# Attention-and-expert kernel: kv products moved into the group of narrow products, spare weight loads put between wide ones

## The chip, the cores and the metric

The kernel runs on one core of one Trainium2 chip. A core has TensorE (PE; its weight loads are shown apart as PEld), VectorE (DVE), ScalarE (ACT), GpSimd (POOL) and SyncE (SP, which mostly issues DMAs). The metric is device time in microseconds of one execution.

## The reference

x has 2048 rows of 640 columns. Two blocks are added to x: linear attention on the normalized rows, and eight rows ("gated rows") that pass through a small gated MLP.

```python
phi = lambda t: jnp.where(t > 0, t + 1, jnp.exp(t)) + 1e-6
pq, pk = phi(q), phi(k)                                  # 32 heads of 20
kv = jnp.einsum("bhsd,bhse->bhde", pk, v)
z = jnp.einsum("bhsd->bhd", pk)
num = jnp.einsum("bhqd,bhde->bhqe", pq, kv)
den = jnp.einsum("bhqd,bhd->bhq", pq, z)[..., None] + 1e-6
attention = (num / den) @ wo

r = x @ w_r                                              # scores of the rows
idx = jnp.argsort(-r, axis=-1)[:, :8]
y = (silu(x[idx] @ w_gate) * (x[idx] @ w_up)) @ w_down * sigmoid(r[idx])
out = x + attention(layernorm(x)) + (x + scatter of y into rows idx)
```

## The kernel before

The 2048 rows are 16 tiles of 128; D = 640 is five chunks of 128. The program is written by hand as one list of calls; each call issues its instructions to its engines in that order, and each engine works its own list in order. Nothing reorders the calls. The stages, by TensorE:

- **Tiles, about 7 to 52 us.** For each tile t: `K(t)` (line 204) makes keys from the transposed normalized rows `xnT` in two halves of 320 columns, five products each. ACT takes exp and relu of a half, DVE joins them into `pk`. `G(t)` (line 245) then multiplies the tile's rows with `pk` and adds up over all tiles in PSUM: for each of five chunks a product of 512 columns, and for four of them one of 128 columns with the same weights. So kv need not have v: kv is worked out later from G and the v part of the weights. From tile 4 on the order is K(t), then G(t-1).
- **q, about 50 to 78 us.** `q_pe(tb, m, bank)` (line 472) makes queries for 512 rows and one fifth m of the columns: five products of 512 columns, weights from `wq` with a column step of five (`by5`), then exp and relu on ACT. There are 4 x 5 groups. `q_fin` joins exp and relu into `pqT` on DVE. Three PSUM banks go round.
- **Between the q groups** stand narrow products, whose weights have 32 columns and which run four side by side in the array (shape 128*32 in the profile): `kv_pe` (line 613) makes kv from G and `wv`; `den` the denominators; `gu_pe` gate and up of the gated rows; `m_tiled` and `m_edge` the products M of kv and wo, left half of the columns first ("left M", h = 0). A head has 20 columns, so heads straddle the 32-row blocks: `kv_ev` (line 629) masks kv on DVE into `kv1` (the main part) and `kv2` (the edge part), and POOL makes copies of kv2 turned by 32, 64 and 96 rows, which `m_edge` reads. `m_ev0` copies left M from PSUM to `Mb`.
- **Gated rows.** `route2` finds the eight rows and lets POOL gather them into `xsT`; `gu_pe`, `gu_act`, `gu_ev` make `hh`; `ht_pe` (line 708) transposes hh and copies it to `hT`; `y_pe` multiplies with w_down.
- **Output, about 78 to 103 us.** `norm` divides pqT by the denominators, `out_mm` multiplies it with `Mb` (lines 735 to 741), `out_ev` adds x and sends the rows out.

A product is two instructions on TensorE, a load of the weights (LDWEIGHTS, shown in PEld) and the product itself (MATMUL).

The calls around kv in the list of before are

```python
    q_pe(0, 3, 1)
    q_fin(0, 2)
    kv_pe(3)
    kv_ev(3)
    q_pe(0, 4, 0)
```

and those of left M, further down, are `m_tiled(0)`, `q_fin(2, 2)`, `den(0, 3, 0)`, `gu_pe(6)`, `m_edge(0)`.

Of the kernel before, what the change touches and what calls it, by code (L numbers as in the profile page):

```python
# [7 lines left out]
P = 128  # L8
# [7 lines left out]
NG = 4  # L16
# [13 lines left out]
BF16 = mybir.dt.bfloat16  # L30
# [4 lines left out]
ALU = mybir.AluOpType  # L35
# [3 lines left out]
def kernel(  # L39
# [13 lines left out]
    pe, dve, act, pool, sp = nc.tensor, nc.vector, nc.scalar, nc.gpsimd, nc.sync  # L53
# [11 lines left out]
    PS = psp.tile([P, 8, 512], F32, name="PS")  # L65
# [16 lines left out]
    zero = st([P, 512], BF16, "zero")  # L82
# [3 lines left out]
    bm2 = st([P, GC], BF16, "bm2")  # L86
# [33 lines left out]
    def warm4(w):  # L120
# [6 lines left out]
        out=ident[:], in_=ident[:], compare_op=ALU.not_equal, fill=1.0,  # L127
# [9 lines left out]
    kv2 = st([P, NG, GC], BF16, "kv2")  # L137
# [65 lines left out]

    def K(t, hs=(0, 1), b=6, ks=range(KC)):
        for h in hs:
            w = HW + h
            for kc in ks:
                pe.matmul(  # L208
                    PS[:, b + h, off(t, h) : off(t, h) + w],
                    lhsT=xnT[:, kc, t * P : (t + 1) * P],  # L210
                    rhs=wkh[h][:, kc, 0:w],
                    start=(kc == 0),
                    stop=(kc == KC - 1),
                )
# [26 lines left out]
    def PHb(t):  # L241
        ek, rk = phis[t]
        dve.scalar_tensor_tensor(out=pk[:, t, :], in0=ek[:], scalar=1.0, in1=rk[:], op0=ALU.min, op1=ALU.add)  # L243

    def G(t, ks=range(KC)):
        for a in ks:
            lhsT = XX[:, t, 0, a * P : (a + 1) * P]
            pe.matmul(  # L248
                PS[:, a, :], lhsT=lhsT, rhs=pk[:, t, 0:512],
                start=(t == 0), stop=(t == T - 1),  # L250
            )
            if a < 4:
                pe.matmul(  # L253
                    PS[:, 5, a * P : (a + 1) * P], lhsT=lhsT, rhs=pk[:, t, 512:D],
                    start=(t == 0 and a == 0), stop=(t == T - 1), skip_group_check=True,
                )
# [215 lines left out]
    def q_pe(tb, m, bank):  # L472
        for kc in range(KC):
            pe.matmul(  # L474
                PS[:, bank, :], lhsT=by5(wq[:, kc, :])[:, m, :], rhs=xnT[:, kc, tb * TBLK : (tb + 1) * TBLK],
                start=(kc == 0), stop=(kc == KC - 1),
            )
        e = tmp.tile([P, D], BF16, tag="ek", name="qe", bufs=3)[:, 0:TBLK]
        r = tmp.tile([P, D], BF16, tag="rk", name="qr", bufs=3)[:, 0:TBLK]
        act.activation(e, PS[:, bank, :], AF.Exp)  # L480
        act.activation(r, PS[:, bank, :], AF.Relu)  # L481
        qst[(tb, m)] = (e, r)
# [41 lines left out]
    Mb = st([P, KC, WS], BF16, "Mb", "wkM")  # L524
    rd_d = drp.tile([2, H, 8 * P], BF16, name="rd_d")

    def q_fin(tb, m):
        e, r = qst[(tb, m)]
        dve.scalar_tensor_tensor(  # L529
            out=pqT[:, m, tb * TBLK : (tb + 1) * TBLK], in0=e, scalar=1.0, in1=r,  # L530
            op0=ALU.min, op1=ALU.add,
        )

    def den(u, bank, o0):
        for m in range(KC):
            for j in range(4):
                o = (4 * u + j) * 2 * P
                pe.matmul(  # L538
                    PS[32 * j : 32 * j + 32, bank, o0 : o0 + 2 * P], lhsT=zm[:, m, :], rhs=pqT[:, m, o : o + 2 * P],
                    start=(m == 0 and o0 == 0), stop=(m == KC - 1), skip_group_check=True,  # L540
                )
# [69 lines left out]
    KW = ((0, 40), (20, 80), (60, 100), (80, 140), (120, GC))  # L611

    def kv_pe(bank):
        for g in range(NG):
            for a in range(KC):
                for b in range(4):
                    w0, w1 = KW[b]
                    pe.matmul(PS[32 * b : 32 * b + 32, bank, g * 64 : g * 64 + w1 - w0],  # L618
                              lhsT=wv[:, a, g * GC + 32 * b : g * GC + 32 * b + 32],
                              rhs=Gs[:, a, g * GC + w0 : g * GC + w1],  # L620
                              start=(a == 0), stop=(a == KC - 1), skip_group_check=True)
        w0, w1 = KW[4]
        for a in range(KC):
            for g in range(NG):
                pe.matmul(PS[32 * g : 32 * g + 32, bank, 256 : 256 + w1 - w0],
                          lhsT=wv[:, a, g * GC + P : (g + 1) * GC], rhs=Gs[:, a, g * GC + w0 : g * GC + w1],
                          start=(a == 0), stop=(a == KC - 1), skip_group_check=True)

    def kv_ev(bank):
        for b in range(4):  # L630
            w0, w1 = KW[b]
            r = slice(32 * b, 32 * b + 32)
            src = PS[r, bank, 0:256].rearrange("p (g c) -> p g c", c=64)[:, :, 0 : w1 - w0]
            dve.tensor_tensor(out=kv1[r, :, w0:w1], in0=src,
                              in1=bm1[r, w0:w1].unsqueeze(1).to_broadcast([32, NG, w1 - w0]), op=ALU.mult)
        w0, w1 = KW[4]
        dve.tensor_tensor(out=kv2[:, 0, w0:w1], in0=PS[:, bank, 256 : 256 + w1 - w0], in1=bm2[:, w0:w1], op=ALU.mult)

        def turned(d, s, n, rows):
            for q in rows:  # L640
                o = (q - 32 * ((d - s) % 4)) % P
                pool.tensor_copy(kv2[o : o + n, d, w0:w1], kv2[q : q + n, s, w0:w1])

        turned(2, 0, 64, (64, 0))
        turned(1, 0, 32, (32, 64, 96, 0))
        turned(3, 1, 64, (64, 0))

    MP = ((0, 2 * P), (2 * P, D))
    MB = (((4, 0), (4, 2 * P), (5, 0), (5, 2 * P), (0, 0)), ((2, 0), (3, 0), (4, 0), (5, 0), (7, 0)))

    def m_tiled(h):
        c0, c1 = MP[h]
        for m, (b, o) in enumerate(MB[h]):
            for g in range(NG):
                pe.matmul(PS[32 * g : 32 * g + 32, b, o : o + c1 - c0], lhsT=by5(kv1[:, g, :])[:, m, :],  # L655
                          rhs=wo1[:, g, c0:c1],
                          start=(o == 0), stop=False, skip_group_check=True)

    def m_edge(h):
        c0, c1 = MP[h]  # L660
        for m in ((0, 2, 4, 1, 3), range(KC))[h]:
            b, o = MB[h][m]
            s = (m // 2, m % NG)[h]
            for g in range(NG):
                r = 32 * ((g - s) % NG)
                pe.matmul(PS[32 * g : 32 * g + 32, b, o : o + c1 - c0], lhsT=by5(kv2[r : r + 32, s, :])[:, m, :],  # L666
                          rhs=wo2[r : r + 32, g, c0:c1],
                          start=False, stop=True, skip_group_check=True)

    def m_ev0(k):  # L670
        if k < 2:
            dve.tensor_copy(Mb[:, 2 * k : 2 * k + 2, 0 : 2 * P], PS[:, 4 + k, :].rearrange("p (m c) -> p m c", m=2))
        else:
            dve.tensor_copy(Mb[:, 4, 0 : 2 * P], PS[:, 0, 0 : 2 * P])

    def m_ev1(eng, m0, m1):
        b, n = MB[1][m0][0], m1 - m0
        d = MB[1][m0 + 1][0] - b if n > 1 else 1
# [10 lines left out]
    hT = st([P, 3, P], BF16, "hT")  # L689

    def gu_pe(b):
        for i, w in enumerate((wg, wu)):
            for kc in range(KC):
                for j in range(4):
                    pe.matmul(PS[32 * j : 32 * j + 32, b + i, P:512], lhsT=xsT[:, kc, :],  # L695
                              rhs=w[:, kc, j * FQ : (j + 1) * FQ],
                              start=(kc == 0), stop=(kc == KC - 1), skip_group_check=True)
# [10 lines left out]
    def ht_pe(bank):  # L708
        pt = PS[:, bank, P : P + 192].bitcast(BF16)
        for k in range(3):  # L710
            pe.transpose(pt[:, k * P : (k + 1) * P], hh[:, k * P : (k + 1) * P], ident[:])
        dve.tensor_copy(hT[:].rearrange("p a b -> p (a b)"), pt[:, 0 : 3 * P])

    def y_pe(b):
        for k in range(F // P):
# [55 lines left out]
    def fix_init():  # L771
        dve.tensor_copy(idxu[:], cols[:, 0:1])
        dve.tensor_scalar(out=idxh[:], in0=cols[:, 0:1], scalar1=float(4 * TF * P), scalar2=None, op0=ALU.subtract)
# [24 lines left out]
    z_ev()  # L798
    for k in range(KC):
        ld(sp, wu[:, k, :], wu_v[:, k, :])  # L800
    q_pe(0, 2, 0)
    q_fin(0, 1)
    q_pe(0, 3, 1)
    q_fin(0, 2)
    kv_pe(3)
    kv_ev(3)
    q_pe(0, 4, 0)
    wd = st([P, F // P, D], BF16, "wd", "pkwd")
    ld(sp, wd[:], B_w_down.rearrange("(fc p) n -> p fc n", p=P))
# [18 lines left out]
    q_fin(2, 0)  # L828
    q_pe(2, 2, 2)
    q_fin(2, 1)  # L830
    m_tiled(0)
    q_fin(2, 2)
    den(0, 3, 0)
    gu_pe(6)
    m_edge(0)
    den_ev(0, 3, 0)
    gu_act(6)
    bcast(0)
    hi_copy()
    gu_ev(6)  # L840
    q_pe(2, 3, 1)
    m_ev0(2)
    q_pe(2, 4, 2)
    ht_pe(3)
    q_fin(2, 3)
    fix_init()
    q_pe(3, 0, 0)
    m_ev0(0)
    q_fin(2, 4)
    m_ev0(1)  # L850
    q_pe(3, 1, 1)
    q_fin(3, 0)
    q_pe(3, 2, 2)
    q_fin(3, 1)
    norm(0, 0, 2)
# [84 lines left out]
```

## Time and profile before

| | us |
|---|---|
| median of 3 runs | 107.11 |
| lowest and highest run | 106.8, 107.3 |
| profiled execution, its time | 106.82 |
| its span in the trace | 105.1 |
| PE busy | 101.2 |
| PEld busy | 63.3 |
| DVE busy | 82.3 |
| ACT busy | 69.3 |
| POOL busy | 17.3 |

The time of an execution is 1.7 us longer than its span, which goes from the first instruction to the last. Busy times are sums of recorded durations, overlaps counted once. The record of a product is longer than the time it holds the array: a row such as 0.38 us for 512 columns overlaps the next product's row by the part that it takes to run through. How far the starts lie apart is the time that counts. A row of the timeline gives start, duration, engine, line, operation, what it writes and reads, shape and number; in brackets how long the engine had been idle, and for what.

### The profile page before, as it was taken

To read this page: it belongs to the slowest core of one execution; us is meant where nothing else is said; L and a number is where in the kernel's file an instruction comes from. 1 tells how busy PE (TensorE), PEld (TensorE's weight loads), DVE (VectorE), ACT (ScalarE), POOL (GpSimd) and SP (SyncE) were. 2 spreads that over 40 slices of the span, in tenths; PEclk is the share of its full clock that TensorE was granted. 3 is DMA by queue.
4 is the path that set the end of the run, shared out by engine and by line. 5 is a ranking of instruction groups with operands and counts; after the bars stand their busy time and mean duration, and the time that the engine had idled before them with its cause. 6 is when DMAs were issued, how large, how long until landed. Compare 5 with 4: busy or idle time off the path is not lost.

```text
span 105.1 us, 2557 instructions
## 1 busy us (share of the span) xinstructions
PE 101.2 (96%) x924; PEld 63.3 (60%) x924; DVE 82.3 (78%) x187; ACT 69.3 (66%) x171; POOL 17.3 (16%) x60
## 2 busy tenths in 40 slices
PE   6999999999999999999999999999999999999980
PEld 3346666666666666667556555655567767777760
DVE  1787999988888897873788985728988997888870
ACT  4289957666666666888596999969993997000000
POOL 7800000620000000000000683300002300000500
DMA  2899937334655765889998999921730125895343
GB/s 76 231 356 386 306 68 62 72 66 90 141 124 115 109 131 128 180 252 354 264 404 264 288 337 378 360 66 50 242 119 9 29 95 200 175 369 205 125 128 125
DMA packets 23024, 19.65 MB, mean 187 GB/s; under 512 B 10595, under 2 KB 21475, under 8 KB 23011
## 3 DMA queue, kind: packets, MB, share of 16 engines
q1 hardware_dynamic: 21880, 19.01, 62.6%
q10 hardware_dynamic: 842, 0.46, 1.8%
q8 instruction: 7, 0.11, 0.5%
q0 software_dynamic: 288, 0.01, 0.3%
q14 instruction: 7, 0.05, 0.2%
HBM read 13.80 MB, written 3.65 MB: 166 GB/s over the span
## 4 chain that ended last, share of the span: by engine, by line
PE 90%; DMA 5%; DVE 1%; issue 1%; ACT 1%; DVEq 0%
PE PS L208 21%; PE PS L474 21%; PE PS L739 20%; PE PS L248 16%; DMA wk<-in_A_wqkv_dram 5%; PE PS L253 3%; PE PS L695 2%; PE PS L655 1%; PE PS L538 1%; PE PS L717 1%; PE PS L267 1%; PE PS L174 1%; PE PS L666 1%; DVE o L752 1%; PE PS L618 1%
## 5 line engine op out<-in xcount | busy, mean ns | idle before, releaser
L208 PE MATMUL PS<-wk,xnT 128*128 128x320 bf16 (+1 forms) x160 | 25.3, 300 | 0.1
L248 PE MATMUL PS<-pk,XX 128*128 128x512 bf16 x80 | 23.5, 379 | 0.0
L474 PE MATMUL PS<-xnT,wq 128*128 128x512 bf16 x100 | 22.6, 380 | 0.0
L739 PE MATMUL PS<-Mb,pqT 128*128 128x320 bf16 (+4 forms) x165 | 22.1, 295 | 0.0
L224 ACT ACTIVATE ek<-PS 128x320 bf16<-128x320 f32 x32 | 14.1, 441 | 9.9 <-PE PS L208 9.9
L739 PEld LDWEIGHTS <-pqT 128*128 128x128 bf16 x165 | 15.9, 98 | 6.4 <-issue 0.3
L208 PEld LDWEIGHTS <-xnT 128*128 128x128 bf16 x160 | 15.3, 98 | 6.6 <-ACT xnT L181 0.2
L474 PEld LDWEIGHTS <-wq 128*128 128x128 bf16 x100 | 11.4, 118 | 9.1 <-issue 0.2
L243 DVE SCALAR_TENSOR_TENSOR pk<-ek,rk 128x640 bf16<-128x640 bf16 x16 | 13.1, 820 | 4.8 <-ACT rk L227 4.5
L529 DVE SCALAR_TENSOR_TENSOR pqT<-qe,qr 128x512 bf16<-128x512 bf16 x20 | 13.5, 683 | 2.1 <-ACT qr L481 2.0
L480 ACT ACTIVATE qe<-PS 128x512 bf16<-128x512 f32 x20 | 12.2, 609 | 3.3 <-PE PS L474 3.3
L253 PE MATMUL PS<-pk,XX 128*128 128x128 bf16 x64 | 14.0, 219 | 0.0
L227 ACT ACTIVATE rk<-PS 128x320 bf16<-128x320 f32 x32 | 14.0, 437 | 0.0
L248 PEld LDWEIGHTS <-XX 128*128 128x128 bf16 x80 | 7.8, 98 | 8.1
L481 ACT ACTIVATE qr<-PS 128x512 bf16<-128x512 f32 x20 | 12.2, 608 | 0.0
L748 DVE TENSOR_TENSOR o<-PS,XX 128x640 bf16<-128x640 f32 x11 | 9.0, 822 | 2.9 <-issue 1.3
L198 ACT ACTIVATE XX<-XX,MR,SR 128x640 bf16<-128x640 bf16 x11 | 9.4, 913 | 0.0
L151 DVE BATCH_NORM_STATS2 stats<-XX 128x6 f32<-128x320 bf16 x16 | 7.4, 461 | 2.2 <-DMA XX<-in_A_x_dram 2.2
L259 POOL MEMSET XX<- 128x1 bf16 x18 | 2.0, 117 | 35.4 <-DVE XX L165 15.2
L165 DVE TENSOR_SCALAR XX<-XX,MVf,SR 128x640 bf16<-128x640 bf16 (+2 forms) x17 | 7.2, 431 | 0.6 <-ACT SR L161 0.6
L154 DVE BATCH_NORM_STATS2 stats<-XX 128x6 f32<-128x320 bf16 x16 | 7.7, 480 | 0.0
L253 PEld LDWEIGHTS <-XX 128*128 128x128 bf16 x64 | 6.3, 98 | 0.8
(113 smaller groups left out, 95.3 us busy)
## 6 DMA issues: line engine op xcount, KB each, us to landing
out_dram<-o SPq DMA_DIRECT2D x15, 160.0 KB, 2.4
XX<-in_A_x_dram SPq DMA_DIRECT2D x3, 640.0 KB, 6.9
wg<-in_B_w_gate_dram SPq DMA_DIRECT2D x5, 384.0 KB, 9.0
wu<-in_B_w_up_dram SPq DMA_DIRECT2D x5, 384.0 KB, 6.2
wd<-in_B_w_down_dram SPq DMA_DIRECT2D x1, 1920.0 KB, 11.1
wv<-in_A_wqkv_dram SPq DMA_DIRECT2D x5, 160.0 KB, 3.0
wq<-in_A_wqkv_dram SPq DMA_DIRECT2D x1, 800.0 KB, 5.3
hi_d<-XX SPq DMA_DIRECT2D x1, 800.0 KB, 4.0
```

The costliest lines, as they stand in the source:

```text
L198: act.activation(XX[:, t, 1, :], XX[:, t, 1, :], AF.Identity, bias=MR[:, t : t + 1], scale=SR1[:, t : t + 1])
L208: pe.matmul(PS[:, b + h, off(t, h) : off(t, h) + w], lhsT=xnT[:, kc, t * P : (t + 1) * P], rhs=wkh[h][:, kc, 0:w], start=(kc == 0), stop=( ...
L224: act.activation(phis[t][0][:, h * HW : (h + 1) * HW], phi_src(t, h, b), AF.Exp)
L227: act.activation(phis[t][1][:, h * HW : (h + 1) * HW], phi_src(t, h, b), AF.Relu)
L243: dve.scalar_tensor_tensor(out=pk[:, t, :], in0=ek[:], scalar=1.0, in1=rk[:], op0=ALU.min, op1=ALU.add)
L248: pe.matmul(PS[:, a, :], lhsT=lhsT, rhs=pk[:, t, 0:512], start=(t == 0), stop=(t == T - 1),)
L253: pe.matmul(PS[:, 5, a * P : (a + 1) * P], lhsT=lhsT, rhs=pk[:, t, 512:D], start=(t == 0 and a == 0), stop=(t == T - 1), skip_group_check= ...
L474: pe.matmul(PS[:, bank, :], lhsT=by5(wq[:, kc, :])[:, m, :], rhs=xnT[:, kc, tb * TBLK : (tb + 1) * TBLK], start=(kc == 0), stop=(kc == KC ...
L480: act.activation(e, PS[:, bank, :], AF.Exp)
L481: act.activation(r, PS[:, bank, :], AF.Relu)
L529: dve.scalar_tensor_tensor(out=pqT[:, m, tb * TBLK : (tb + 1) * TBLK], in0=e, scalar=1.0, in1=r, op0=ALU.min, op1=ALU.add,)
L739: pe.matmul(PS[:, b, o : o + c1 - c0], lhsT=pqT[:, kc, t * P : (t + 1) * P], rhs=Mb[:, kc, c0:c1], start=(kc == 0), stop=(kc == KC - 1))
```

## The change

Four things, by the list of calls and the functions:

1. `pad(n)` issues n weight loads of 128 zero columns with no product of their own. One stands ahead of each half of K(t) for t > 3, one behind each 512-column product of G(t) for t > 0, and one behind each product of q_pe for the blocks tb < 3.
2. `kv_pe` and `kv_ev` move from behind q(0,3) to behind q(2,3), directly ahead of `den`, `gu_pe`, `m_tiled(0)` and `m_edge(0)`; `m_tiled(0)` now stands behind `gu_pe`. The PSUM banks of some q groups, of kv and of the last block of left M change with it.
3. In `kv_ev` the edge part kv2 is masked first, POOL turns by 32 first, and `m_edge(0)` reads only the unturned kv2 and the one turned by 32.
4. `ht_ev` (the copy to hT) is apart from `ht_pe`, one q group stands between gate/up and `ht_pe` more than before, and the copies of left M (`m_ev0`) stand ahead of it.

```diff
     def K(t, hs=(0, 1), b=6, ks=range(KC)):
         for h in hs:
+            if t > 3:
+                pad(1)
             w = HW + h
...
+    def pad(n):
+        for _ in range(n):
+            pe.ldweights(zero[:, 0:P])
+
     def G(t, ks=range(KC)):
         for a in ks:
...
+            if t:
+                pad(1)
             if a < 4:
...
                 start=(kc == 0), stop=(kc == KC - 1),
             )
+            if tb < 3:
+                pad(1)
         e = tmp.tile([P, D], BF16, tag="ek", name="qe", bufs=3)[:, 0:TBLK]
...
     def kv_ev(bank):
+        w0, w1 = KW[4]
+        dve.tensor_tensor(out=kv2[:, 0, w0:w1], in0=PS[:, bank, 256 : 256 + w1 - w0], in1=bm2[:, w0:w1], op=ALU.mult)
+
         for b in range(4):
...
-        w0, w1 = KW[4]
-        dve.tensor_tensor(out=kv2[:, 0, w0:w1], in0=PS[:, bank, 256 : 256 + w1 - w0], in1=bm2[:, w0:w1], op=ALU.mult)
-
...
+        w0, w1 = KW[4]
+        turned(1, 0, 32, (32, 64, 96, 0))
         turned(2, 0, 64, (64, 0))
-        turned(1, 0, 32, (32, 64, 96, 0))
         turned(3, 1, 64, (64, 0))
 
     MP = ((0, 2 * P), (2 * P, D))
-    MB = (((4, 0), (4, 2 * P), (5, 0), (5, 2 * P), (0, 0)), ((2, 0), (3, 0), (4, 0), (5, 0), (7, 0)))
+    MB = (((4, 0), (4, 2 * P), (5, 0), (5, 2 * P), (1, 0)), ((2, 0), (3, 0), (4, 0), (5, 0), (7, 0)))
...
-            s = (m // 2, m % NG)[h]
+            s = (m // 2 % 2, m % NG)[h]
...
-    kv_pe(3)
-    kv_ev(3)
     q_pe(0, 4, 0)
...
-    m_tiled(0)
+    q_pe(2, 3, 0)
     q_fin(2, 2)
+    kv_pe(1)
+    kv_ev(1)
+    q_fin(2, 3)
     den(0, 3, 0)
     gu_pe(6)
+    m_tiled(0)
     m_edge(0)
     den_ev(0, 3, 0)
     gu_act(6)
     bcast(0)
     hi_copy()
     gu_ev(6)
-    q_pe(2, 3, 1)
+    q_pe(2, 4, 2)
     m_ev0(2)
-    q_pe(2, 4, 2)
+    q_pe(3, 0, 0)
     ht_pe(3)
-    q_fin(2, 3)
-    fix_init()
-    q_pe(3, 0, 0)
     m_ev0(0)
     q_fin(2, 4)
-    m_ev0(1)
+    ht_ev(3)
+    fix_init()
     q_pe(3, 1, 1)
     q_fin(3, 0)
+    m_ev0(1)
     q_pe(3, 2, 2)
```

On TensorE, where one tile's G ends and the next K begins (G reads `XX` and `pk`, K reads `xnT` and `wk`), there stood before

```order
L253 MATMUL PS<-pk,XX 128x128
L248 LDWEIGHTS XX
L248 MATMUL PS<-pk,XX 128x512
L208 LDWEIGHTS xnT
L208 MATMUL PS<-wk,xnT 128x320
```

and now stands

```order
L254 LDWEIGHTS XX
L254 MATMUL PS<-pk,XX 128x512
L249 LDWEIGHTS zero
L261 LDWEIGHTS XX
L261 MATMUL PS<-pk,XX 128x128
L254 LDWEIGHTS XX
L254 MATMUL PS<-pk,XX 128x512
L249 LDWEIGHTS zero x2
L210 LDWEIGHTS xnT
L210 MATMUL PS<-wk,xnT 128x320
```

A zero load stands between a product and the next product's own load, and two of them where G's last chunk meets K; the rows have become 2002 from 1840.

On TensorE, at the new place of kv (the last q group ahead of it, then kv from `Gs` and `wv`), there now stands

```order
L249 LDWEIGHTS zero
L482 LDWEIGHTS wq
L482 MATMUL PS<-xnT,wq 128x512
L249 LDWEIGHTS zero
L628 LDWEIGHTS wv
L628 MATMUL PS<-Gs,wv 32x40
L628 LDWEIGHTS wv
L628 MATMUL PS<-Gs,wv 32x60
```

Before, a q product stood directly ahead of its next load, and behind the kv products another q group followed; now den follows.

On VectorE, around the masks of kv (`kv1`, `kv2`; the numbers behind the names are buffers, L529 and L539 are `q_fin`, L587 and L597 the search of `route2`, L705 and L716 `gu_ev`), there stood before

```order
L634 TENSOR_TENSOR kv1_121<-PS_68,bm1_84 32x4x40
L634 TENSOR_TENSOR kv1_121<-PS_68,bm1_84 32x4x60
L637 TENSOR_TENSOR kv2_122<-PS_68,bm2_85 128x40
L529 SCALAR_TENSOR_TENSOR pqT_72<-qe_868,qr_869 128x512
L529 SCALAR_TENSOR_TENSOR pqT_72<-qe_991,qr_992 128x512
L587 MAX k8_813<-krow_812 1x8
```

and now stands

```order
L539 SCALAR_TENSOR_TENSOR pqT_72<-qe_1217,qr_1218 128x512
L641 TENSOR_TENSOR kv2_122<-PS_68,bm2_85 128x40
L647 TENSOR_TENSOR kv1_121<-PS_68,bm1_84 32x4x40
L647 TENSOR_TENSOR kv1_121<-PS_68,bm1_84 32x4x60
L647 TENSOR_TENSOR kv1_121<-PS_68,bm1_84 32x4x40
L647 TENSOR_TENSOR kv1_121<-PS_68,bm1_84 32x4x60
L539 SCALAR_TENSOR_TENSOR pqT_72<-qe_1232,qr_1233 128x512
L716 TENSOR_TENSOR hh_929<-PS_68,hs_928 128x384
```

The masks have moved from ahead of the search for the gated rows to just ahead of `gu_ev`, with kv2 in front. On POOL the eight turning copies moved in the same way, from ahead of the gather into `xsT` to behind it.

More of the change, by code (lines that the diff above doesn't have):

```diff
@@ L673, in m_ev0 @@
         else:
-            dve.tensor_copy(Mb[:, 4, 0 : 2 * P], PS[:, 0, 0 : 2 * P])
+            dve.tensor_copy(Mb[:, 4, 0 : 2 * P], PS[:, 1, 0 : 2 * P])
     def m_ev1(eng, m0, m1):
@@ L711, in ht_pe, with ht_ev @@
             pe.transpose(pt[:, k * P : (k + 1) * P], hh[:, k * P : (k + 1) * P], ident[:])
-        dve.tensor_copy(hT[:].rearrange("p a b -> p (a b)"), pt[:, 0 : 3 * P])
+    def ht_ev(bank):
+        dve.tensor_copy(hT[:].rearrange("p a b -> p (a b)"), PS[:, bank, P : P + 192].bitcast(BF16))
     def y_pe(b):
@@ L800 @@
         ld(sp, wu[:, k, :], wu_v[:, k, :])
-    q_pe(0, 2, 0)
+    q_pe(0, 2, 1)
     q_fin(0, 1)
-    q_pe(0, 3, 1)
+    q_pe(0, 3, 2)
     q_fin(0, 2)
-    kv_pe(3)
-    kv_ev(3)
     q_pe(0, 4, 0)
```

## The prediction

> **What bounds the kernel now.** I read the page's span and busy shares first, then the chain that ended last, then the stretches of the span, to see whether any stage leaves TensorE a gap.
>
> ```profile
> span 105.1 us, 2557 instructions
> PE 101.2 (96%) x924; PEld 63.3 (60%) x924; DVE 82.3 (78%) x187; ACT 69.3 (66%) x171; POOL 17.3 (16%) x60
> ...
> PE 90%; DMA 5%; DVE 1%; issue 1%; ACT 1%; DVEq 0%
> ```
>
> ```profile
> 20.00:30.00 10.00, 10.00 (x74) 6.33 (x72) 7.94 (x21) 7.05 (x23) 1.85 (x11) 1.00 0.43 94
> ...
> 56.60:66.40 9.80, 9.80 (x49) 5.17 (x53) 8.12 (x22) 8.91 (x20) 5.36 (x14) 1.00 1.00 329
> 81.00:101.00 20.00, 20.00 (x148) 14.29 (x147) 16.91 (x27) 7.65 (x10) 2.99 (x2) 1.00 0.53 166
> ```
>
> The second view has one row a stretch: its length, then busy time of PE, PEld, DVE, ACT and POOL, the granted clock, DMA. PE is busy in every microsecond of each, at clock 1.00, and 90% of the chain is PE. So whatever lengthens PE's own stream between 7 and 101 us goes straight into the end, and only what shortens that stream helps. The chain in order of time shows how full the stream is:
>
> ```profile
> 49.06 0.84 PE PS L267 x15
> 49.90 1.08 PE PS L474 x5
> ```
>
> A product of 128 columns takes 0.84/15 = 0.056 us, one of 512 columns 1.08/5 = 0.216 us. The difference, 160 ns for 384 columns, is 0.417 ns a column, so each product has some 2.7 ns that are not columns. Nothing else is idle in the stream. Every product has a weight load of its own, and where it runs is seen in the timeline of G, PE first, PEld below:
>
> ```profile
> 42.26 0.38 PE L248 MATMUL PS<-pk,XX 128*128 128x512 bf16 x1
> 42.48 0.22 PE L253 MATMUL PS<-pk,XX 128*128 128x128 bf16 x1
> 42.53 0.38 PE L248 MATMUL PS<-pk,XX 128*128 128x512 bf16 x1
> ```
>
> ```profile
> 42.26 0.10 PEld L253 LDWEIGHTS <-XX 128*128 128x128 bf16 x1
> 42.48 0.10 PEld L248 LDWEIGHTS <-XX 128*128 128x128 bf16 x1
> ```
>
> The load of the next product starts at the very time the product in front starts (42.26, 42.48): one load ahead, never two, and the 0.056 us of a 128-column product are enough for it.
>
> **The spare loads.** G has 15 tiles x 5 = 75, K 12 tiles x 2 = 24, q 15 groups x 5 = 75: 174 loads. No row shows two loads with no product between them, so the price has to be bounded. The rows that bear on it are those of loads that nothing covered:
>
> ```profile
> 8.82 0.11 PEld L174 LDWEIGHTS <-XX 128*128 128x128 bf16 x2 [0.25 <-DVE XX L165]
> 8.83 0.23 PE L174 MATMUL PS<-ident,XX 128*128 128x128 bf16 x1
> ```
>
> ```profile
> 56.51 0.16 PEld L474 LDWEIGHTS <-wq 128*128 128x128 bf16 x2
> ```
>
> ```profile
> 56.51 0.41 PE L474 MATMUL PS<-xnT,wq 128*128 128x512 bf16 x1
> ```
>
> ```profile
> L474 PEld LDWEIGHTS <-wq 128*128 128x128 bf16 x100 | 11.4, 118 | 9.1 <-issue 0.2
> L248 PEld LDWEIGHTS <-XX 128*128 128x128 bf16 x80 | 7.8, 98 | 8.1
> ```
>
> After a wait, the two loads from XX span 0.11 us, one alone is 0.098, so the second (which follows its product's start) began some 12 ns after the first: an uncovered XX load costs 12 ns. After the kv products the two wq loads span 0.16, one is 0.118, and the first product is recorded with 0.41 instead of 0.38 us: an uncovered wq load costs about 35 ns (its columns lie five apart).
>
> Lowest price: the spare load and the real one both run under the 0.216 us product in front; nothing is added, and at the very best the 2.7 ns beside the columns vanish: 0 to -0.4 us. Highest: each real load is laid bare with its whole recorded duration, 99 x 0.098 + 75 x 0.118 = 18.6 us. Between them: the spare load takes the one place ahead, the real load must wait until the product in front is through, and each pad costs the real load's uncovered price. Of the 75 q pads 72 stand in front of a wq load (the others before XX, the transposed keys and kv): 72 x 0.035 = 2.5 us. The 99 of G and K stand before XX and xnT loads (also unstrided, 98 ns): 99 x 0.012 = 1.2 us; where two stand together, the second zero load is laid bare too, at the same 12 ns. Sum 3.7 us. I take this middle value, since the timeline shows one load ahead and no case of two, and since the 12 and 35 ns are this kernel's own prices for a load that waits for an idle array.
>
> The Trainium skill, TensorE: Matmul & The Clock Gate, section LDWEIGHTS (loading the stationary operand), prices a load at its columns over 1.2, which is 107 ns for 128 columns; by that the 174 loads would be an estimated 18.6 us. The trace disagrees: a whole load fits under a 0.056 us product.
>
> Is there cover for 3.7 us? Not on PE. ACT would have to be the bound of the q stage for a slower PE to be free, and it isn't:
>
> ```profile
> 57.83 0.60 ACT L480 ACTIVATE qe<-PS 128x512 bf16<-128x512 f32 x1 [0.83 <-PE PS L474]
> ...
> 63.69 0.57 ACT L480 ACTIVATE qe<-PS 128x512 bf16<-128x512 f32 x1
> ...
> 64.65 0.57 ACT L480 ACTIVATE qe<-PS 128x512 bf16<-128x512 f32 x1
> ```
>
> ACT needs 64.65 - 63.69 = 0.96 us a group, PE 1.08, and ACT waits for PE at 57.83. So PE's delay goes through.
>
> **The kv products moved to 66 us.** Now they stand alone between full-size products:
>
> ```profile
> 55.09 0.59 PE L474 MATMUL PS<-xnT,wq 128*128 128x512 bf16 x2
> 55.61 0.81 PE L618 MATMUL PS<-Gs,wv 128*32 128x40 bf16 x80
> 56.23 0.35 PE L625 MATMUL PS<-Gs,wv 128*32 128x40 bf16 x20
> ```
>
> ```profile
> 65.83 0.59 PE L474 MATMUL PS<-xnT,wq 128*128 128x512 bf16 x2
> 66.35 0.75 PE L655 MATMUL PS<-wo,kv 128*32 128x256 bf16 x20
> 66.93 0.72 PE L538 MATMUL PS<-pqT,zm 128*32 128x256 bf16 x20
> ```
>
> The last q product starts at 55.09 + 0.59 - 0.38 = 55.30 and streams until 55.52; kv starts at 55.61: 0.09 us of change of tile shape. The last kv product starts at 56.23 + 0.35 - 0.19 = 56.39 and is through by 56.41; the next full-size load is at 56.51 and costs 35 ns more: 0.13 us. Joined to den, gate/up and left M (all 128*32), kv pays the first change, in left M's place (also 0.09: 66.26 to 66.35), and not the second: -0.22 us. The TensorEngine Tiling (Array Packing) page of the Trainium skill (Key Properties) says a change of tiling mode drains the array; the 0.09 and 0.13 us agree.
>
> What waits for kv there? DVE and POOL now:
>
> ```profile
> 56.67 1.49 DVE L634 TENSOR_TENSOR kv<-PS,bm 32x160 bf16<-32x160 f32 x4
> 58.19 0.20 DVE L637 TENSOR_TENSOR kv<-PS,bm 128x40 bf16<-128x40 f32 x1
> ```
>
> ```profile
> 58.52 3.61 POOL L642 COPY kv<-kv 64x40 bf16<-64x40 bf16 x8 [13.68 <-DVE kv L637]
> 62.33 0.94 POOL L599 COPY xsT<-xnT 128x5 bf16 x2 [0.20 <-ACT qr L481]
> ...
> 67.30 0.21 POOL L599 COPY xsT<-xnT 128x5 bf16 x1 [0.48 <-issue]
> ```
>
> ```profile
> 67.56 0.28 PEld L695 LDWEIGHTS <-xsT 128*32 128x32 bf16 x12 [0.19 <-POOL xsT L599]
> ```
>
> ```profile
> 67.11 0.55 PE PS L538 x19
> 67.65 1.72 PE PS L695 x40
> ```
>
> Left M's first load waits for kv1: from kv's last product some 0.2 us to DVE (an estimate: the q group after kv ends at 56.51 + 0.035 + 5 x 0.216 = 57.63, and ACT takes it up at 57.83), 0.1 to 0.2 for kv2, 1.5 for the four kv1 rows: 1.8 to 1.9 us. PE has den and gate/up meanwhile, 0.55 + 1.72 = 2.27 us: 0.4 us to spare. The edge products need only kv2 and the first four, smaller, of its eight copies: at most 0.4 + 3.61 / 2 = 2.2 us after kv, against 2.27 and left M's 0.58 (66.35 to 66.93) of PE work. The POOL copies stood ahead of the gather of the eight rows (62.33 to 67.51), and gate/up's first load waited 0.19 us for the gather; with the copies behind it the gather can start some 3 us earlier. What of the 0.19 lay beside den's last products is not in a row, so between 0 and -0.19 I take half: -0.1 us. The later group does not wait for ACT: 0.83 us of ACT's idle at 57.83 is gone, but 1.08 against 0.96 keeps it up. Sum of the move: -0.3 us.
>
> **Left M copied ahead; hT apart.** The copies on DVE are the same, in another order. The transposes of hh stand one q group (1.08 us) later, and the bank that q(3,1) takes over is read out by a copy that stands a q group ahead of it. What hides this is DVE's slack ahead of the first output products, which wait for norm:
>
> ```profile
> 76.22 0.81 DVE L564 TENSOR_TENSOR pqT<-pqT,R 128x1280 bf16<-128x1280 bf16 x1
> ```
>
> ```profile
> 77.58 0.55 PE PS L739 x5
> ```
>
> Norm is done at 77.03, 0.55 us early. PE comes 0.3 us sooner, so the cost is 0; without that cover it would be what DVE is late beyond 0.25 us.
>
> **Sum.** 3.7 - 0.3 = +3.4 us on this execution's 106.82 us (span 105.1 and 1.7 around it): 110.2. The runs' median, 107.11, is 0.3 above the profiled one, so 110.5 us.
>
> **Rivals.** (1) The loads are free: the second overwrites the first while the product in front still streams. For it: PEld is busy 63.3 of 105 us, and 0.216 us holds two loads of 0.056 with room. Against it: no row shows two ahead. Then only the move is left: 107.11 - 0.3 = 106.8, and 106.4 if the 2.7 ns went too. It decides as soon as the second load may start before the product ends: the kernel is then not slower. The same page of the Trainium skill, Step-by-step: what each phase is for, says loads are pulled ahead of products in flight when they go to the background weight buffer; whether a second one may, it does not say, and no run here shows it yet. (2) The uncovered load costs more than its 12 or 35 ns, since the array must empty first, as at a change of tile shape (0.09 to 0.13 us): 174 x 0.05 to 0.107 gives +8.7 to +18.6, so 115.5 to 125.4 us. Against it: at 8.82, after an idle array, it was 12 ns. (3) The loads are free, but left M waits: one pqT row (0.7 us) that comes to stand late ahead of them on DVE turns the 0.4 us to spare into a wait of 0.3, and the move gains nothing: 107.1.
>
> **The numbers.** Middle price 0.47, free 0.36, dear 0.13, free with a wait 0.04. Faster than 0.5% (0.54 us; less than that a few runs cannot tell from no change) is only the better third of the free case: 0.12. Within it: the rest of that and (3): 0.26. Slower: 0.62, the middle and the dear price and a remainder. The range reaches from the free case, 106.3, to 112.5, where 12 ns have become 30; the dear case is left out. The middle price alone would be 109.5 to 111.5.
>
> **What the profile after would show.** By the forecast: in K and G the zero load starts with the product in front and the real one only after that has ended; G of one tile, now 5 x 0.216 + 4 x 0.056 = 1.30 us, takes about 0.06 more; a q group takes 1.25 instead of 1.08. If the loads are free, these stay 1.30 and 1.08. The kv products directly ahead of den, with no gap, and left M starting without a wait on DVE would show the move right. A PE wait ahead of left M, or in front of q(3,1), would show my slack wrong.

## The result and the profile after

The changed kernel takes 107.88 us in the median of 4 runs (107.60 to 108.41), the kernel before 106.95 on the same chip (106.33 to 107.30): a ratio of 1.0121, with an interval of 1.0093 to 1.0150 (the medians alone give 1.0087, 0.93 us). It is slower, as forecast, but by 0.9 to 1.3 us where 3.4 were forecast, and for other reasons. All ratios here leave out runs that took over 1.5% longer than the fastest of their kernel. The profiled run took 107.84 us with a span of 106.0; the span before was 105.1. These 0.9 us are what the two traces can account for.

The page of the changed kernel, its span, its busy shares and its chain by engine:

```profile
span 106.0 us, 2723 instructions
PE 100.6 (95%) x916; PEld 70.6 (67%) x1098; DVE 82.6 (78%) x187; ACT 68.7 (65%) x171; POOL 16.0 (15%) x60
...
q8 instruction: 8, 0.13, 0.6%
...
PE 69%; DMA 12%; DVE 9%; ACT 3%; issue 2%; SPq 2%; DVEq 0%
```

PE is busy for no longer than before (100.6 us against 101.2), although 174 more weight loads are in PEld's count. The chain is no longer 90% PE: DMA has 12% of it. So the loss lies in waits for transfers and not in TensorE's stream.

The timeline of G after the change, the weight loads first and then the products:

```profile
42.36 0.10 PEld L254 LDWEIGHTS <-XX 128*128 128x128 bf16 x1
42.50 0.10 PEld L249 LDWEIGHTS <-zero 128*128 128x128 bf16 x1
42.54 0.10 PEld L261 LDWEIGHTS <-XX 128*128 128x128 bf16 x1
42.72 0.10 PEld L254 LDWEIGHTS <-XX 128*128 128x128 bf16 x1
```

```profile
42.50 0.38 PE L254 MATMUL PS<-pk,XX 128*128 128x512 bf16 x1
42.72 0.49 PE L261 MATMUL PS<-pk,XX 128*128 128x128 bf16 x2
43.04 0.38 PE L254 MATMUL PS<-pk,XX 128*128 128x512 bf16 x1
```

At 42.50 a product starts, and the zero load with it. The real load follows 0.04 us later, at 42.54, while the product still streams, and the next product starts 0.22 us after the first, as before. The chain shows the same at three later points:

```profile
41.30 1.36 PE PS L210 x10
...
49.30 0.84 PE PS L275 x15
...
52.57 1.08 PE PS L482 x5
```

The same G products that began at 49.06 before (quoted in the prediction) begin at 49.30: 0.24 us late. K at 41.30 is 0.24 late too (41.06 before), and 52.57 stands against 52.33. K of tile 4 starts 0.23 us late (17.14 against 16.91, shown below), so the 35 us from there on, with 94 spare loads by the trace, add nothing. The 0.24 us came in one place, K of tile 4. The timelines of PE there, before and after:

```profile
16.70 0.38 PE L248 MATMUL PS<-pk,XX 128*128 128x512 bf16 x1
16.91 1.53 PE L208 MATMUL PS<-wk,xnT 128*128 128x320 bf16 x10
```

```profile
16.39 0.38 PE L254 MATMUL PS<-pk,XX 128*128 128x512 bf16 x1
17.14 1.26 PE L210 MATMUL PS<-wk,xnT 128*128 128x320 bf16 x8 [0.37 <-DMA xnT<-XX]
```

After, TensorE was 0.3 us ahead here and then waited 0.37 us for the transposed tile. What this transfer met is in the DMA queues of the stretch from 14 to 15 us, before and then after (packets, MB, share of 16 engines' time):

```profile
q1 hardware_dynamic: 350, 0.09, 43.6%
```

```profile
q1 hardware_dynamic: 499, 0.13, 204.9%
q8 instruction: 1, 0.02, 7.2%
```

A packet of the instruction queue, 16 KB of an engine's own program, falls among the pieces of the transposition (it starts at 14.35 us by the trace); 7.2% of 16 engines in 1 us is 1.15 us of one engine. The time of a piece goes from 0.020 us on average (43.6% of 16 us, over 350 pieces) to 0.066 (204.9%, over 499; the times overlap, so that they can add up to more than 100%), and the slowest piece by the trace from 0.06 to 1.47 us. Before, the first such packet came at 16.1 us, with the transposition over: the 32 packets of 4 bytes that close it end at 15.5 us, after the change at 16.3 us.

The other two differences stand later. The start of the first output block, PE before, then DVE and PE after:

```profile
77.42 0.71 PE L739 MATMUL PS<-Mb,pqT 128*128 128x256 bf16 x5
```

```profile
76.99 0.82 DVE L574 TENSOR_TENSOR pqT<-pqT,R 128x1280 bf16<-128x1280 bf16 x1 [0.81 <-DMA R<-rd_d]
```

```profile
76.54 1.03 PE L482 MATMUL PS<-xnT,wq 128*128 128x512 bf16 x4
77.87 0.72 PE L752 MATMUL PS<-Mb,pqT 128*128 128x256 bf16 x5 [0.30 <-DVE pqT L574]
```

The reciprocal denominators R come late; before, DVE did this at 76.22 and waited for nothing. The last of the four q products starts at 76.54 + 1.03 - 0.38 = 77.19, so the output products could have started at 77.40, and started at 77.87: 0.47 us. At the end of the program SyncE waits for a transfer that nobody waited for before; the waits of its queue after 95 us:

```profile
SPq L949 <- DMA out_dram<-ysb,idxu: 0.8, 1, 0.8
```

And the indirect add of the eight rows, on POOL, before and after:

```profile
98.49 1.55 POOL L766 DMA_INDIRECT out_dram<-ysb,idxu  x1 [16.05 <-DMA out_dram<-o]
```

```profile
100.90 1.54 POOL L779 DMA_INDIRECT out_dram<-ysb,idxu  x1 [17.72 <-DMA out_dram<-o]
```

It waits for an output write, is issued 2.4 us later and is the last to land. By the landing signals in the trace of after, fifteen of the sixteen parts of that write are there by 98.7 us, the sixteenth at 100.6. The last three output rows on DVE, before and after:

```profile
101.60 0.94 DVE L752 TENSOR_TENSOR o<-PS,XX 128x320 bf16<-128x320 f32 x3
```

```profile
102.06 0.94 DVE L765 TENSOR_TENSOR o<-PS,XX 128x320 bf16<-128x320 f32 x3
```

From their start to the end of the span it is 106.0 - 102.06 = 3.94 us, before 105.1 - 101.60 = 3.50: 0.44 us.

The move of the kv products did what was forecast. The group on PE after:

```profile
66.64 0.81 PE L628 MATMUL PS<-Gs,wv 128*32 128x40 bf16 x80
67.26 0.35 PE L635 MATMUL PS<-Gs,wv 128*32 128x40 bf16 x20
67.43 0.74 PE L548 MATMUL PS<-pqT,zm 128*32 128x256 bf16 x20
...
69.61 0.73 PE L666 MATMUL PS<-wo,kv 128*32 128x256 bf16 x20
70.27 0.53 PE L677 MATMUL PS<-wo,kv 32*32 32x256 bf16 x20
70.73 1.49 PE L482 MATMUL PS<-xnT,wq 128*128 128x512 bf16 x5
```

kv, den, gate/up, left M and the edge follow each other without a gap, and TensorE, 0.24 us late at 52 us, has made that up by the q products behind the group. So the 0.9 us of the profiled pair are +0.24 (K waits for its tile), -0.27 (the kv move), +0.47 (R late) and +0.44 (the last add late): +0.88.

### The profile page after: what moved, and what is told of

The parts are those of the page before. It is cut to its first block, busy times and chain, and to the rows that moved or that the text cites. A ratio compares the mean times of both kernels' runs of the same rounds, so it can differ in the third digit from the quotient of the medians.

```text
span 106.0 us, 2723 instructions
## 1 busy us (share of the span) xinstructions
PE 100.6 (95%) x916; PEld 70.6 (67%) x1098; DVE 82.6 (78%) x187; ACT 68.7 (65%) x171; POOL 16.0 (15%) x60
## 4 chain that ended last, share of the span: by engine, by line
PE 69%; DMA 12%; DVE 9%; ACT 3%; issue 2%; SPq 2%; DVEq 0%
PE PS L752 18%; PE PS L210 16%; PE PS L482 14%; PE PS L254 12%; DMA xnT<-XX 4%; PE PS L261 3%; DMA R<-rd_d 3%; DMA rd_d<-rden 2%; DMA XX<-in_A_x_dram 2%; SPq L103 2%; DVE XX L165 2%; DVE pk L245 1%; DVE stats L151 1%; DVE stats L154 1%; PE PS L548 1%
## 5 line engine op out<-in xcount | busy, mean ns | idle before, releaser
L254 PE MATMUL PS<-pk,XX 128*128 128x512 bf16 x75 | 22.7, 379 | 0.0
L249 PEld LDWEIGHTS <-zero 128*128 128x128 bf16 x174 | 16.3, 98 | 5.1
L539 DVE SCALAR_TENSOR_TENSOR pqT<-qe,qr 128x512 bf16<-128x512 bf16 x20 | 13.5, 684 | 2.7 <-ACT qr L491 2.7
L254 PEld LDWEIGHTS <-XX 128*128 128x128 bf16 x80 | 7.8, 98 | 5.6
```

Source lines behind the costliest of these rows:

```text
L249: pe.ldweights(zero[:, 0:P])
L254: pe.matmul(PS[:, a, :], lhsT=lhsT, rhs=pk[:, t, 0:512], start=(t == 0), stop=(t == T - 1),)
L539: dve.scalar_tensor_tensor(out=pqT[:, m, tb * TBLK : (tb + 1) * TBLK], in0=e, scalar=1.0, in1=r, op0=ALU.min, op1=ALU.add,)
```

## The experiments

Each was timed against the kernel before on the same chip; that kernel's median there was 106.63 to 106.77 us. "The pads" are the spare zero loads.

**The pads alone: pads_only.** The kernel before, with the three pad hunks of the change and nothing else.

```diff
+            if t > 3:
+                pad(1)
...
+            if t:
+                pad(1)
...
+            if tb < 3:
+                pad(1)
```

> The kernel before with the 174 zero loads and nothing moved. Theory A (each zero load and the load behind it both run under the 0.216 us product in front, so the loads cost nothing, and the changed kernel is late by other things): ratio 0.997 to 1.003, G and q products spaced 0.216 us. Rival B (the loads delay something, such as the transposes or the copies by DMA): 1.006 to 1.015.

Measured: 107.90 us, ratio 1.0101 (1.0068 to 1.0135). The whole loss is here, but not in the loads' own time: K of tile 4 waits, and the output products then begin at 77.97 us against 77.42 before, 0.55 later; the last add is issued at 101.18, and SyncE waits 0.9 us for it. So the time is B's, outside A's range, and what A said of the loads holds. PE, then the add:

```profile
17.45 0.99 PE L210 MATMUL PS<-wk,xnT 128*128 128x320 bf16 x6 [0.75 <-DMA xnT<-XX]
```

```profile
101.18 1.54 POOL L776 DMA_INDIRECT out_dram<-ysb,idxu  x1 [18.18 <-DMA out_dram<-o]
```

**The move alone: move_only.** The changed kernel without the three pad hunks.

> The changed kernel without any zero load. Theory A: ratio 1.008 to 1.016, as for the whole change, with norm again waiting some 0.8 us for R at about 77 us and TensorE waiting 0.3 to 0.5 us ahead of the first output product. Rival B: 0.995 to 1.002, no such wait.

Measured: 107.02 us (106.23 to 108.22), ratio 1.0003 (0.9973 to 1.0034): no change, as B expected, and a wide spread. K of tile 4 doesn't wait. The 0.27 us are gained by kv and lost again a little later. PE's timeline:

```profile
69.41 0.73 PE L660 MATMUL PS<-wo,kv 128*32 128x256 bf16 x20
70.08 0.32 PE L671 MATMUL PS<-wo,kv 32*32 32x256 bf16 x8
70.99 0.42 PE L671 MATMUL PS<-wo,kv 32*32 32x256 bf16 x12 [0.59 <-issue]
```

TensorE stands for 0.59 us in the middle of twenty equal products, where the profile shows no semaphore that is waited for. More on this under move_q. The norm doesn't wait for R here, as A had expected it to. The trace is of a run of 107.42 us; whether the faster runs have the stop too is not known.

**The pair again: after_again, before_again.** Both kernels unchanged, as a second pair of traces.

> The changed kernel once more, for a second trace on the same chip as the two halves. Theory A: 1.009 to 1.015, with the wait for R at 77 us, and the last add of the gated rows issued near 101 us. If the wait for R or the late add belongs to the one trace alone, they are missing here.

> The kernel before once more, for a second trace. Theory A: no wait of norm for R, R landed with 0.3 us or more to spare, the last add issued near 98.5 us; time within 0.5% of the runs of before.

Measured: 107.91 us, ratio 1.0110 (1.0068 to 1.0152), and 106.67. The waits return at their places: K of tile 4 waits 0.35 us, the last add is issued at 101.0 us (98.3 in the kernel before), and the instruction packets come within 1 us of where they came in the first pair. So the waits come back with the program. Their sizes do not quite: K of tile 4 starts at 17.16 us against 16.64 here, 0.52 us late where the first pair had 0.23, and the tail is only some 0.2 us longer (105.75 - 102.04 against 104.95 - 101.45).

**A few loads at the start: early8.** If the loads cost nothing but lengthen the program, then eight of them at a place where TensorE is idle anyway, far from G, K and q, must do harm too. The kernel before with

```diff
     warm4(512)
+    for _ in range(8):
+        pe.ldweights(zero[:, 0:P])
```

> The kernel before with only eight zero loads, put into the start, where TensorE waits 1.3 us for the first rows. Theory F (the zero loads cost TensorE nothing; they lengthen its program, which is brought in by packets of 16 KB, and each packet holds one of the 16 DMA engines for 1.1 us, so it matters which transfer is under way when one comes): the packet of 16.1 us comes near 14.3 us, among the pieces of the transposed tile 4, and K(4) waits 0.3 to 0.8 us for it near 17 us; ratio 1.002 to 1.007. Rival P (weight loads that run beside a product slow the transfers or the copies by themselves): 0.998 to 1.002, no wait, since the eight run alone.

Measured: 107.52 us, ratio 1.0081 (1.0057 to 1.0104). Eight loads of at most 0.1 us, issued before the first tile is there, cost 0.9 us, a little more than expected (1.002 to 1.007). The DMA queues from 14 to 15 us, and PE:

```profile
q1 hardware_dynamic: 494, 0.13, 217.6%
q8 instruction: 1, 0.02, 8.1%
```

```profile
17.37 0.99 PE L210 MATMUL PS<-wk,xnT 128*128 128x320 bf16 x6 [0.61 <-DMA xnT<-XX]
```

The packet has moved from 16.1 to 14.3 us, onto the transposition, and K of tile 4 waits 0.61 us; the output products start 0.62 us late (78.04). The median loses 0.9 us where the two spans differ by 0.6: the profiled run of before, 106.82 us, lies 0.17 above its median here (106.65), that of early8, 107.42, 0.10 below its own.

Why eight rows move the packet by almost 2 us is argued from the program's order, not shown. G(2) begins some 170 instructions into TensorE's program and needs pk(2). If the packet is asked for a few rows behind that point, it has to wait for pk(2); with five to eight more rows ahead, it is asked for before. In the traces pk(2) is done at 14.8 to 15.3 us. The first packet starts 1.0 to 1.4 us after that in the seven traces with no row added ahead of G(2), 0.4 to 0.6 us before it in after, after_again, pads_only and early8, and 0.3 us after it in early_mm4 and gk_pads. The last two have as many rows there as early8 and pads_only, so the number of rows is not all that sets the moment.

**Four products in their place: early_mm4.** Eight instructions at the same place that are not spare loads: four products of 4 columns, each with its own load, into a bank that is not in use there.

```diff
+    for _ in range(4):
+        pe.matmul(PS[:, 7, 0:4], lhsT=zero[:, 0:P], rhs=zero[:, 0:4], start=True, stop=True)
```

> The kernel before with four products of zeros, four columns each, in the start: eight instructions as in early8, but four of them products. Theory F (only the length of the program counts): as early8, the packet near 14.3 us, K(4) waits 0.4 to 0.8 us, ratio 1.004 to 1.011. If it was the spare loads as such that cost, not the instructions: half of early8's loss or none, 0.998 to 1.004.

Measured: 107.80 us, ratio 1.0071 (1.0044 to 1.0098; one run, at 120.57 us, stands alone); K of tile 4 waits 0.83 us. The packet starts at 15.5 us, not at 14.3 as expected, but still ahead of the transposition's last pieces: the packets that close it end at 17.0 us. Four products with their loads do the same harm as eight spare loads; it is the number of instructions, not their kind.

**Forty loads at the start of the changed kernel: after_early40.** The same loop with `range(40)`, in the changed kernel: it moves all packets, the first one ahead of the transposition.

> The changed kernel with 40 more zero loads in the start, so that every later packet of the program comes 40 instructions sooner. Theory F: the packet of 14.3 us comes near 12 us and the one of 97.6 us near 95 us; K(4) doesn't wait, the last add is issued at 98.3 to 99.2 us instead of 101; ratio 0.997 to 1.006. Rival P: 1.009 to 1.016, as the changed kernel, both waits still there.

Measured: 107.28 us (106.69 to 109.45), ratio 1.0045 (1.0019 to 1.0071): forty instructions more, and 0.6 us less than the changed kernel. The first packet starts at 13.8 us and lasts until 15.2, so that it still holds back part of the transposition (the packets that close it end at 16.5 us), but K of tile 4 doesn't wait, and the last add is issued at 99.1. The runs fall into two heaps (106.7 to 107.4, and 108.5 to 109.5); the ratio and the trace are those of the faster heap, so what the others wait for stays open.

**Which pads: gk_pads and q_pads.** The kernel before with the first two pad hunks (99 loads), or with the third alone (75).

> The kernel before with the zero loads of G and K alone (99). Theory F: the wait ahead of K(4) is there; the packet of 93.7 us has moved to about 87 us and none comes near 97, so the last add is issued at 98 to 99.7 us; ratio 1.002 to 1.007. Rival P: 99/174 of the loss, 1.005 to 1.007, with both the wait and a late add.

> The kernel before with the zero loads of q alone (75). Theory F: the packet of 16.1 us stays, K(4) doesn't wait; the packet of 93.7 us comes near 88 us, the last add is issued at 98 to 99 us; ratio 0.998 to 1.002. Rival P: 75/174 of the loss, 1.003 to 1.006.

Measured: 107.53 us, ratio 1.0063 (1.0038 to 1.0088), and 106.76 us, ratio 1.0008 (0.9985 to 1.0031). The 75 loads of q, for which most of the price was forecast, cost nothing. With G's and K's the packet starts at 15.5 us, and K of tile 4 waits 0.89 us.

**How many loads fit: depth.** The kernel before with q's pads alone, three loads ahead of each product in the first block, eight in the second, one in the third.

```diff
+            if tb < 3:
+                pad((3, 8, 1)[tb])
```

> The kernel before with zero loads in q alone: three behind each product of the first 512 rows, eight for the second, one for the third. In the changed kernel a zero load and the next load start 0.042 us apart. If loads follow one another at that pace under the product in front, products stay 0.216 us apart with one and with three (four loads, 0.17 us) and are 0.34 to 0.40 us apart with eight (nine loads). If only the first load ran under the product, three would already give 0.26 us or more.

Measured: 110.28 us in one run, span 108.6. PE in the first block, then PEld in the second:

```profile
53.17 2.32 PE L478 MATMUL PS<-xnT,wq 128*128 128x512 bf16 x10
```

```profile
60.06 0.12 PEld L478 LDWEIGHTS <-wq 128*128 128x128 bf16 x1
60.07 0.40 PEld L247 LDWEIGHTS <-zero 128*128 128x128 bf16 x8
60.42 0.12 PEld L478 LDWEIGHTS <-wq 128*128 128x128 bf16 x1
60.43 0.40 PEld L247 LDWEIGHTS <-zero 128*128 128x128 bf16 x8
60.78 0.12 PEld L478 LDWEIGHTS <-wq 128*128 128x128 bf16 x1
```

With three spare loads the ten products still start (2.32 - 0.38) / 9 = 0.216 us apart, as without any. With eight, the real loads are 0.36 us apart: nine loads, 0.04 us each. A load takes 0.04 us of the load path, and four of them were free under a product of 512 columns; by an estimate, 0.216 / 0.04, five would be. The 0.1 us that each shows in PEld overlap. The sum agrees: 25 products of the second block at 0.36 - 0.216 us more are 3.6 us, and the span is 3.5 longer.

The Trainium skill's page TensorE: Matmul & The Clock Gate gives the columns over 1.2 (section LDWEIGHTS (loading the stationary operand)), 107 ns, and in its next section, on weight-path modes, a fast load that the compiler chooses for 128 columns of bf16, about twice as fast when measured. That would be an estimated 53 ns; the 40 ns measured here are less. No run here shows which mode the loads were in.

**The move with q's pads: move_q.** The changed kernel without the pads of K and G: 99 rows fewer than after, 75 more than move_only.

> The changed kernel with the zero loads of q alone: kv moved, no load ahead of row 163 of TensorE's program. Theory F: the packet stays at 16 us, K(4) doesn't wait, the last add at 98 to 99.5 us; the rest depends on whether the packet that falls into the narrow products at 66 to 71 us is late, as in the move alone (0.6 us): ratio 0.995 to 1.003. Rival P: 1.003 to 1.007.

Measured: 109.43 us (108.52 to 111.01), ratio 1.0229 (1.0184 to 1.0274): the slowest of all with one load a product, though neither part costs anything alone; neither expectation had that. PE's timeline:

```profile
68.69 0.81 PE L702 MATMUL PS<-wu,xsT 128*32 128x384 bf16 x13
70.61 0.51 PE L702 MATMUL PS<-wu,xsT 128*32 128x384 bf16 x7 [1.10 <-issue]
```

Later DVE waits for R:

```profile
91.98 0.82 DVE L570 TENSOR_TENSOR pqT<-pqT,R 128x1280 bf16<-128x1280 bf16 x1 [1.14 <-DMA R<-rd_d]
```

At 70.6 us TensorE has stood for 1.1 us, again without a semaphore, and in other products than in move_only: gate/up here, the edge there. Counted in TensorE's program it is the same place. Ahead of the stop stand 607 loads and 606 products in move_only (each product has one load, and the loads are recorded without a gap), 642 loads and 571 products in move_q: 1213 instructions in both. The rows given with the change, 1840 and 2002, are fewer than the instructions, since equal neighbours stand there as one row (`zero x2`); by the traces TensorE's program has 924 loads and 924 products before, 1848 in all, and 2022 after. The packets fit the count: 1213 less and plus multiples of 256 are 189, 445, 701, 957, 1213, 1469, 1725 and 1981, which a program of 1848 instructions passes seven times and one of 2022 eight times, and every kernel here has seven or eight packets accordingly.

The narrow products run through the 256 instructions from 957 to 1213 in some 3.2 us (in move_only from 66.9 to 70.1), 80 a microsecond, where the tile stage has some 14. The packet that was asked for near 957 starts at 68.64 us in move_only and at 68.28 in move_q, and TensorE goes on at 70.99 and 70.61, 2.3 us later in both. After the change the same packet starts at 64.10 and the place is reached at 67.46, 3.4 us later, without a stop. So TensorE had run through its program faster than the next piece became usable. That a piece needs these 2.3 us is worked out from the two stops, not shown. The trace of move_q is of its fastest run; what makes the others up to 2.5 us longer stays open.

The Trainium skill's page Runtime: NRT & Kernel Launch, section Instruction fetch mechanics, says that an engine's program is streamed in blocks of 16 KiB, 256 instructions, each fetched while the one in front runs, and that crossing a block is mostly hidden. Blocks and count agree with these traces; hidden it was not: TensorE stood 0.59 and 1.10 us here, and waited for transfers beside which a packet lay.

**The packets put elsewhere: tuned.** The changed kernel, with G's pads only from tile 4 on, and two of them from tile 5: the first packet then comes at 16 us again, and only one block begins within the narrow products, as in the changed kernel.

```diff
-            if t:
-                pad(1)
+            if t > 3:
+                pad(1 if t == 4 else 2)
```

> The changed kernel with G's loads from tile 4 on, one there and two from tile 5 on: no load ahead of row 163, and behind it as many rows as in the changed kernel with 40 more in front, whose narrow products ran without a gap and whose last packet came at 94 us. Theory F: the packet stays at 16 us, K(4) doesn't wait, no gap in the narrow products, the first output product 0.1 to 0.4 us sooner than before, the last add at 98 to 99.3 us; ratio 0.994 to 1.001, though it has 55 zero loads more than the changed kernel less 15. Rival P: 1.011 to 1.018.

Measured: 106.46 us in 12 runs (106.12 to 107.00), ratio 0.9979 (0.9962 to 0.9995), span 104.7. It has 214 spare loads, 40 more than the changed kernel, and it is some 1.3 to 1.4% faster than that (by the ratios, 1.0110 and 1.0121) and, by an interval that just excludes no change, 0.2% faster than the kernel before. PE and POOL:

```profile
16.80 1.53 PE L210 MATMUL PS<-wk,xnT 128*128 128x320 bf16 x10
...
69.94 0.53 PE L677 MATMUL PS<-wo,kv 32*32 32x256 bf16 x20
...
77.08 0.71 PE L752 MATMUL PS<-Mb,pqT 128*128 128x256 bf16 x5
```

```profile
98.39 1.55 POOL L779 DMA_INDIRECT out_dram<-ysb,idxu  x1 [15.74 <-DMA out_dram<-o]
```

None of the waits is there, the output products start 0.34 us earlier than before, and the last add goes out where it did before. At the q group behind the last G TensorE is 0.09 us ahead of before (52.24 against 52.33), so 0.25 of the 0.34 us come from the group of narrow products. This is about the -0.3 us of the move, come through at last.

## Why the prediction was right and wrong, point by point

- **The spare loads, +3.7 us: this step failed.** It read "one load ahead, never two" off rows that never had two loads to show, and from it that the real load must wait until the product in front is through. The trace after and depth show that it follows the spare one after 0.04 us, under the running product. By the prediction's own sign, a q group still takes 1.08 us, not 1.25. The term is 0. The 12 and 35 ns were true prices of a load behind an idle array, but none of the 174 loads stood there. Rival (1), that the loads are free, was right about the loads; its time of 106.8 us was not, because of what follows.
- **What the sum lacked: the length of TensorE's own program.** More rows move the moments at which 16 KB pieces of program are fetched. At K of tile 4 this costs 0.24 us in the profiled pair, 0.5 in the second pair, and waits of up to 0.9 us in other kernels: early8 and early_mm4 show it with eight instructions of either kind, and tuned shows its absence with 214 loads. The page of before had the row that would have led there, `q8 instruction: 7, 0.11, 0.5%`; by its share it was too small to read on.
- **The direction was right by accident.** The kernel is slower by 0.9 to 1.3 us, and none of it is the term that carried the forecast.
- **The kv move, -0.3 us: right.** 0.27 us gained, with kv directly ahead of den, no change of tile shape between, and left M without a wait on DVE. The rival of a pqT row late ahead of left M did not occur. Not foreseen is that so many narrow products in a row outrun the fetch of the program: in move_only the gain is lost in that way.
- **Copies and hT apart, cost 0 under 0.55 us of slack: the order was right, the cover was not.** The copies and the transposes made nothing late. But the slack that was to cover them is gone, because R came late. Two things make that up. R's copies were issued at 71.7 us instead of 71.2, as den's evaluation on ACT starts at 68.2 instead of 67.7: K's wait is 0.24 us of this, the rest comes from den's products, which stand behind kv's now (in move_only, without K's wait, it starts at 68.0). And the copies took 3.4 us to land (median of the four; 3.3 in after_again) instead of 2.2. A packet of program lies beside them, at 74.2 us. In six more traces a copy of R took over 2.5 us, and each has a packet beside it. In q_pads and move_q it is a copy of a later block, with packets at 87.7 and 89.2 us; that of move_q took 4.0 us, and DVE waited 1.1 us for it. In tuned, with a packet from 71.45 to 72.3 us, none took over 2.3. The write of hi_d, which begins in the same stretch after the change, is not needed for a slow copy: in move_q it is issued at 74.65 us, 13 us ahead of the slow one. That the packet is the cause rests on this coincidence; no run moves that packet alone.
- **The tail: not in the prediction at all.** 0.44 us come from the last add, which waits for an output write beside which a packet lies at 97.5 to 98.0. pads_only has the same packet at 98 and the same late add; after_early40 and tuned, whose eighth packet comes at 94.8 to 94.9, issue theirs at 99.1 and 98.4. It needs the eighth piece of program, which gk_pads, with 1947 instructions, does not have: its add, at 99.8, is as late as its first output products (78.60, 1.2 us late) make it, and not the last to land. How much of the 0.9 to 1.3 us the tail has over all runs is open.

## What to carry to other kernels

Before an edit that only adds instructions is called free, count the rows of that engine's program and look at where the instruction queue's packets fall: a transfer of small pieces that an engine waits for, or a dense run of short instructions, is where eight rows cost 0.7 to 0.8% here. A result that moves by this much with the place of a few idle instructions says nothing on the edit itself; shift the program by some rows at a harmless place and measure again before judging. And a load that is seen one ahead shows what was asked of the hardware, not what it can do: two or three extra loads in one stage answer that directly.

## What the runs showed of the hardware that was not expected

- A spare weight load of 128 columns costs 0.04 us of the load path; four loads lie hidden under a product of 512 columns, nine do not (depth).
- One packet of 16 KB of program keeps one DMA engine of sixteen busy for some 1.2 us (7.2% and 8.1% of sixteen engines in 1 us). Among the pieces of a transposition it made TensorE wait 0.35 to 0.9 us (after, after_again, pads_only, early8, early_mm4, gk_pads).
- TensorE can stand for its own program: 0.59 and 1.10 us, behind instruction 1213 of two different programs, among products that start 0.02 to 0.04 us apart.
- What stays open: what divides the runs of after_early40 into heaps and spreads those of move_only and move_q over 2 us, what besides the number of rows sets the moment of the first packet, and how the loss of the tail and of R varies from run to run.
